# A retention and FFN kernel: the first 13 steps of pass 1 issued from a fixed list of small pieces

## The chip, the core and the metric

The kernel runs on one core of one Trainium2 chip. The metric is device time in microseconds (us) of one execution, lower is better. The kernel before takes 897.48 us (median of 3 runs, 896.96 to 897.90).

The engines are named as the profile names them: PE (TensorE; PEld is its weight load), DVE (VectorE), ACT (ScalarE), POOL (GpSimd) and SP (SyncE, which here only issues transfers). All times inside the profile are counted from the span's start.

## The reference, cut to what matters

```python
# B, H, S, D = 4, 8, 576, 64
scores = (q @ k.T) / sqrt(D)                        # retention, per batch and head
ret = scores * where(i >= j, gamma[h] ** (i - j), 0)
x = (ret @ v).transpose(0, 2, 1, 3).reshape(2304, 512)
h = x @ w_in                                        # 512 -> 2048
g = where(h >= 1, h, where(h <= -1, 0, (h + 1) ** 2 / 4))
x = g @ w_out                                       # 2048 -> 512
out = (x @ w_a) * (x @ w_b) @ w_out2                # 512 -> 1536 -> 512
```

q, k and v are float32. The weights are float64 and reach the kernel as 64-bit integers, so each weight tile is converted to float32 on the chip.

## The kernel before, in words

**Retention** runs over 18 chunks of 128 positions. For chunk c the kernel loads queries, keys and values (tile u, 1 MB in two transfers of 512 KB from SP, four buffers), scales the values by a decay on POOL (`prepare`), forms eight score products on PE into two PSUM banks and masks them on DVE into tile ret (`score`), then multiplies ret by the values into the bank po, adds the carried state's part to the same bank, and forms the chunk's own addition to the state in the bank pn (`output`). `evacuate` multiplies po by a decay into xf (DVE), rounds xf into the high part of x (ACT), adds pn to state (DVE, or an ACT copy where a batch begins) and subtracts to get the low part of x (DVE). A wait is written nowhere: it follows from tiles, buffers and banks.

**The first FFN layer** works on six blocks of 384 positions (three chunks each) and 16 slices of 128 hidden units, cut into three passes. Pass 1 covers slices 0 to 2 for block 0, 0 to 3 for block 1, 0 to 5 for the others. A step is one (block, slice): 12 products into the bank ph (`l1`), the activation on ACT, ACT, DVE, ACT, DVE (`act1`: t, t, t, high part of g, low part of g), and, one step later, 12 products into four accumulator banks (`l2`). Every product is done in three parts, high by high, low by high and high by low, on pairs of tiles that hold the two parts.

**Weights** come as raw tiles of 128 x 512 x 8 bytes (512 KB). `begin` does two ACT operations on a raw tile and two on DVE (L149, L152), `finish` one integer addition, and `split` an ACT copy (the high part) and a DVE subtraction (L168, the low part). The addition of the first two tiles is on DVE (L159, custom operation), that of the others on POOL (L159).

**The order.** Up to step 24 the five engines issue in the order in which the Python code calls these functions (`manual_schedule`); from step 25 on a scheduler decides. Before the change, a short sequence of calls does chunks 0 to 2 and the first tiles, and then the loop over steps calls `rounds_to` (whole chunks: score, then output and evacuate), the step's 12 products, `act1` with the next tile's conversion in its middle, and the previous step's `l2`. PSUM has four banks of tag ps, handed out in turn to s, s, po, pn and ph, so a product waits until the bank's last reader four allocations back is done; and four accumulator banks.

At the start, DVE zeroes a tile, four products on it run on PE, and the tables (con: masks and key decays; tab: four pieces of 6 KB) are loaded from the ACT queue; `table` spreads tab over the partitions with products and ACT copies into qdec.

Of the kernel before, what the change touches and what calls it, by code (L numbers as in the profile page):

```python
# [9 lines left out]
F32 = mybir.dt.float32  # L10
# [66 lines left out]
def retention_ffn_kernel(  # L77
# [29 lines left out]
    def mm(o, l, r, start, stop, goes_on=False):  # L107
        nc.tensor.matmul(o, l, r, start=start, stop=stop, skip_group_check=goes_on)  # L108
# [29 lines left out]
    def begin(raw, t=None):  # L138


        w = raw.bitcast(U32).rearrange("p (n t) -> p t n", t=2)
        low, high = w[:, 0, :], w[:, 1, :]
        r = raw.bitcast(I32).rearrange("p (n t) -> p t n", t=2)[:, 0, :]
        if t is None:
            t = conv_pool[0].tile([P, 512], F32, tag="conv", name="conv")
        tu = t.bitcast(U32)
        nc.scalar.activation(t, high.bitcast(F32), AF.Abs, scale=2.0 ** -112)
        nc.scalar.activation(r, low, AF.Copy, scale=2.0 ** -29)  # L148
        nc.vector.tensor_scalar(  # L149
            out=tu, in0=tu, scalar1=3, scalar2=None, op0=ALU.logical_shift_left  # L150
        )
        nc.vector.scalar_tensor_tensor(  # L152
            out=tu, in0=high, scalar=0x80000000, in1=tu, op0=ALU.bitwise_and, op1=ALU.bitwise_or
        )
        return t, r

    def finish(t, r, adder=None):
        ti = t.bitcast(I32)
        (adder or nc.vector).tensor_tensor(out=ti, in0=ti, in1=r, op=ALU.add)  # L159
        return t  # L160

    def convert(raw, t=None, adder=None):
        return finish(*begin(raw, t), adder)

    def split(t, pool):
        wt = pool.tile([P, 2, 512], F32R, tag="w", name="w")
        nc.scalar.copy(wt[:, 0, :], t)
        nc.vector.tensor_sub(wt[:, 1, :], t, wt[:, 0, :].bitcast(F32))  # L168
        return wt


    stream = []
# [235 lines left out]
    def score(c):  # L408

        mask = masks[len(parts_of(c)) - 1]  # L410
        t = units[c]
        f = rets[c] = a2.tile([P, 2, DM], F32, tag="ret", name="ret")
        s = [ps.tile([P, 512], F32, tag="ps", name=f"s{h}") for h in range(2)]
        for e in range(NCC):
            for h in range(2):
                rows = slice(D * h, D * h + D)
                mm(
                    s[h][:, P * e:P * e + P], t[rows, K0 + P * e:K0 + P * e + P],
                    t[rows, Q0 + P * e:Q0 + P * e + P], True, True,
                )  # L420
        for h in range(2):
            masked[0] = nc.vector.tensor_mul(  # L422
                f[:, h].rearrange("p (e i) -> p e i", e=NCC),
                s[h].rearrange("p (e i) -> p e i", e=NCC),
                mask.unsqueeze(1).to_broadcast([P, NCC, P]),
            )
# [36 lines left out]
    def evacuate(c, po, pn):  # L463

        x = get_x(c // CPB)
        o = slice(c % CPB * P, c % CPB * P + P)
        fv = po.rearrange("p (c i) -> p c i", c=NCC)
        f = a2.tile([P, DM], F32, tag="xf", name="xf").rearrange("p (c i) -> p c i", c=NCC)
        nc.vector.tensor_mul(f, fv, qdec[:, :, c * P % S:c * P % S + P])
        fv = f  # L470
        cast[0] = nc.scalar.copy(x[:, 0, :, o], fv)
# [8 lines left out]
        nc.vector.tensor_sub(x[:, 1, :, o], fv, x[:, 0, :, o].bitcast(F32))  # L480

    masked, cast = [None], [None]
    loaded, ready, scored, done = [0], [0], [0], [0]

    def load_next(limit):
# [17 lines left out]
    def output_next():  # L503

        c = done[0]
        load_next(c + CHUNKS)
        prepare_next(c + 3)
        evacuate(c, *output(c))
        done[0] += 1

    def rounds_to(n):
# [28 lines left out]
    def act1(ph, between=lambda: None):  # L540
        t = tpool.tile([P, TB], F32, tag="t", name="t")
        g = gpool.tile([P, 2, TB], F32R, tag="g", name="g")
        nc.scalar.activation(t, ph[:, :TB], AF.Relu, bias=0.5, scale=0.5)  # L543
        nc.scalar.activation(t, t, AF.Square)  # L544
        nc.vector.scalar_tensor_tensor(  # L545
            out=t, in0=t, scalar=1.0, in1=ph[:, :TB], op0=ALU.min, op1=ALU.max
        )
        between()
        anchor[:] = [
            nc.scalar.copy(g[:, 0, :], t),  # L550
            nc.vector.tensor_sub(g[:, 1, :], t, g[:, 0, :].bitcast(F32)),  # L551
        ]
# [4 lines left out]
    def accs(n):  # L557
        return [acc.tile([P, 512], F32, tag=f"acc{m}", name=f"acc{m}") for m in range(n)]

    def l2(step):  # L560
# [10 lines left out]
        if last:  # L571
            y_out(i, b)

    yin = {}
# [590 lines left out]
```

## Time and profile before

| | |
|---|---|
| median of 3 runs | 897.48 us (896.96 to 897.90) |
| the profiled execution's own time | 895.57 us |
| its span in the profile | 893.8 us |
| PE busy | 877.4 us, 98% of the span, 5716 products |
| PEld / DVE / ACT / POOL busy | 862.2 / 592.1 / 447.3 / 92.9 us |
| DMA over the span | 238.16 MB, 266 GB/s on average |

The profiled execution lies 1.9 us below the median of the runs, and 1.8 us of it lie around the span. Matmuls are pipelined, and the profile models their ends: a busy PE is not PE at its peak, and a product at half clock counts as busy too. The granted clock (PEclk) is 1.00 at 2.4 GHz and 0.50 at 1.2 GHz. An instruction's releaser is the one whose semaphore came last.

### The profile page before, as it was taken

The page shows a single profiled execution, that of the slowest core. Times are in us where ns is not written, and L with a number is a line of the kernel's source. Part 1 is how long each engine was busy: PE and PEld are TensorE (multiplying, and loading weights), DVE is VectorE, ACT ScalarE, POOL GpSimd, SP SyncE. Part 2 cuts the span into 40 slices and gives each one's busy share as a digit, 9 for nine tenths or more (in the row PEclk, how much of TensorE's full clock was granted, in tenths as well). Part 3 has the DMA queues.
Part 4 walks back from the last instruction along what each step waited for, and adds up shares of the span by engine and source line. Part 5 has one row for each costly group of instructions (what it writes and reads, how often), then busy time and mean ns, then how long its engine had stood idle before and what let it go on. Part 6 is the DMA issues. An engine that isn't in the chain of part 4 may idle for free.

```text
span 893.8 us, 15170 instructions
## 1 busy us (share of the span) xinstructions
PE 877.4 (98%) x5716; PEld 862.2 (96%) x5716; DVE 592.1 (66%) x1075; ACT 447.3 (50%) x903; POOL 92.9 (10%) x113
## 2 busy tenths in 40 slices
PE   8799999999999999999999999999999999999998
PEld 5689999999999999999999999999999999999998
DVE  3787776657777779877888966655245376245465
ACT  3444554456666577656667544443233353333253
POOL 1334433201100101111000000000000000000000
PEclk9799999999999999999999999999999999999999
DMA  8867644455787889998988997869556489857584
GB/s 325 310 245 274 246 170 173 154 188 204 246 312 286 297 278 311 304 382 321 341 292 290 406 398 265 283 224 338 192 200 213 141 282 405 335 179 235 171 285 157
DMA packets 81224, 238.16 MB, mean 266 GB/s; under 512 B 8408, under 2 KB 35160, under 8 KB 78848
## 3 DMA queue, kind: packets, MB, share of 16 engines
q1 hardware_dynamic: 71328, 196.64, 61.7%
q0 software_dynamic: 9664, 40.37, 13.1%
q8 instruction: 45, 0.74, 0.3%
q10 hardware_dynamic: 160, 0.19, 0.1%
q14 instruction: 27, 0.22, 0.1%
HBM read 175.83 MB, written 61.34 MB: 265 GB/s over the span
## 4 chain that ended last, share of the span: by engine, by line
PE 88%; DVE 5%; DMA 3%; issue 2%; ACT 2%; SPq 0%; POOL 0%; POOLq 0%; DVEq 0%; ACTq 0%
PE acc L108 31%; PE ph L108 21%; PE qx L108 16%; PE qy L108 8%; PE late L108 4%; PE qz L108 4%; PE po L108 2%; PE s L108 1%; DVE w L168 1%; DMA b<-yf 1%; DVE ret L422 1%; DVE conv L152 1%; DMA con<-in_const 1%; DMA tab<-in_const 0%; DMA yin<-y 0%
## 5 line engine op out<-in xcount | busy, mean ns | idle before, releaser
L108 PE MATMUL acc<-g,w 128*128 128x384 f32 x1296 | 247.1, 334 | 0.0
L108 PE MATMUL ph<-x,w 128*128 128x384 f32 x1152 | 223.6, 339 | 7.5 <-DVE ret L422 4.8
L108 PEld LDWEIGHTS acc<-g,w 128*128 128x128 f32 x1296 | 226.5, 188 | 0.1
L108 PEld LDWEIGHTS ph<-x,w 128*128 128x128 f32 x1152 | 203.5, 190 | 9.7 <-issue 5.5
L108 PE MATMUL qx<-tx,w 128*128 128x384 f32 x864 | 164.5, 334 | 0.5 <-DVE keep L688 0.5
L108 PEld LDWEIGHTS qx<-tx,w 128*128 128x128 f32 x864 | 151.0, 188 | 0.8 <-DVE keep L688 0.8
L666 ACT COPY keep<-qx 128x384 f32<-128x384 f32 x126 | 59.8, 481 | 141.9 <-PE qx L108 136.4
L545 DVE SCALAR_TENSOR_TENSOR t<-t,ph 128x384 f32<-128x384 f32 x96 | 52.9, 553 | 54.0 <-ACT t L544 53.6
L108 PE MATMUL qy<-tx,w 128*128 128x384 f32 x432 | 86.5, 335 | 0.0
L543 ACT ACTIVATE t<-ph 128x384 f32<-128x384 f32 x96 | 47.0, 489 | 72.0 <-PE ph L108 71.7
L108 PE MATMUL acc<-sp,w 128*128 128x384 f32 x432 | 77.5, 334 | 0.0
L108 PEld LDWEIGHTS qy<-tx,w 128*128 128x128 f32 x432 | 75.8, 188 | 0.6 <-ACT keep L666 0.3
L108 PEld LDWEIGHTS acc<-sp,w 128*128 128x128 f32 x432 | 75.1, 188 | 0.0
L550 ACT CAST g<-t 128x384 fp32r<-128x384 f32 x96 | 48.9, 510 | 39.4 <-DVE t L545 38.9
L551 DVE TENSOR_TENSOR g<-t,g 128x384 fp32r<-128x384 f32 x96 | 53.4, 556 | 21.3 <-ACT g L550 21.1
L759 DVE TENSOR_TENSOR sp<-gb,sp 128x768 fp32r<-128x768 f32 x42 | 40.2, 956 | 22.2 <-ACT sp L758 21.9
L544 ACT ACTIVATE t<-t 128x384 f32<-128x384 f32 x96 | 50.4, 526 | 2.6
L758 ACT CAST sp<-gb 128x768 fp32r<-128x768 f32 x42 | 35.2, 837 | 32.6 <-PE acc L108 18.8
L701 DVE TENSOR_TENSOR keep<-keep 128x384 f32<-128x384 f32 x36 | 20.1, 558 | 47.4 <-ACT keep L666 47.4
L148 ACT ACTIVATE raw<-raw 128x512 int32<-128x512 uint32 x68 | 45.6, 670 | 1.7 <-DMA raw<-in_moe_w_in 1.3
L108 PE MATMUL qz<-tx,w 128*128 128x384 f32 x216 | 43.4, 334 | 0.0
L688 DVE TENSOR_TENSOR keep<-qz,keep 128x384 f32<-128x384 f32 x36 | 20.1, 558 | 30.0 <-PE qz L108 29.1
(99 smaller groups left out, 993.0 us busy)
## 6 DMA issues: line engine op xcount, KB each, us to landing
w<-q SPq DMA_DIRECT2D x126, 512.0 KB, 5.3
q<-q SPq DMA_DIRECT2D x42, 512.0 KB, 5.8
w<-o SPq DMA_DIRECT2D x42, 512.0 KB, 4.6
u<-in_qkv SPq DMA_DIRECT2D x36, 512.0 KB, 6.1
x<-xd SPq DMA_DIRECT2D x12, 1536.0 KB, 8.0
raw<-in_moe_w_out POOLq DMA_DIRECT2D x18, 512.0 KB, 7.1
yin<-y SPq DMA_DIRECT2D x48, 192.0 KB, 4.2
xd<-x POOLq DMA_DIRECT2D x5, 1536.0 KB, 9.5
```

The lines of the kernel that those rows point to most:

```text
L108: nc.tensor.matmul(o, l, r, start=start, stop=stop, skip_group_check=goes_on)
L148: nc.scalar.activation(r, low, AF.Copy, scale=2.0 ** -29)
L543: nc.scalar.activation(t, ph[:, :TB], AF.Relu, bias=0.5, scale=0.5)
L544: nc.scalar.activation(t, t, AF.Square)
L545: nc.vector.scalar_tensor_tensor(out=t, in0=t, scalar=1.0, in1=ph[:, :TB], op0=ALU.min, op1=ALU.max)
L550: nc.scalar.copy(g[:, 0, :], t),
L551: nc.vector.tensor_sub(g[:, 1, :], t, g[:, 0, :].bitcast(F32)),
L666: nc.scalar.copy(t, o[:, :HT])
L688: nc.vector.tensor_add(self.c11, z[:, :HT], self.c11)
L701: nc.vector.tensor_add(self.c22, self.c22, self.s5)
L758: nc.scalar.copy(t[:, 0], b)
L759: nc.vector.tensor_sub(t[:, 1], b, t[:, 0].bitcast(F32))
```

## The change

The work of the first 13 steps (blocks 0, 1 and 2) and of the chunks that go with it is cut into pieces, and a table of 251 tokens says in which order the pieces are issued. Each engine gets its own pieces in that order. A token is a letter and a number: r and u load raw tile or chunk; V, S, P are prepare, score and output of a chunk; X, C, O are the three parts of evacuate (xf and the high part of x; state; low part of x); A, B, f or F, H, W are the parts of a weight tile's conversion (ACT pair; DVE pair; addition on POOL or DVE; high part; low part); L, T, U, G, J, Z are a step's first products, two ACT operations, DVE minimum and maximum, high part of g, low part of g, and second products; Q is table, Y the store of a block's accumulators, E the store of x. After the table the old loop goes on with step 13, with 12 chunks output, 13 scored, 14 prepared and 16 loaded. The loop of before stands at the same point when step 11's second products end.

Three things are changed besides: eight warm-up products instead of four, on a tile of which only one half is zeroed; tab is loaded from the POOL queue instead of ACT's; and the additions of tiles 0 and 1 go to POOL, those of tiles 8 and 10 to DVE.

```diff
-ON_POOL, BY_HAND = 12, 2
+ON_POOL = 12
+ORDER = """
+    r0 u0 r1 u1 u2 r2 u3 A0 B0 V0 S0 A1 B1 Q0 f0 S1 P0 u4 r3 X0 H0 V1 C0 W0 O0 S2 P1 u5
+    r4 r5 X1 V2 A2 C1 f1 B2 V3 O1 H1 f2 Q1 S3 P2 u6 r6 V4 X2 C2 S4 H2 O2 P3 u7 A3 W1 X3
...
 def begin(raw, t=None):
     nc.scalar.activation(t, high.bitcast(F32), AF.Abs, scale=2.0 ** -112)
     nc.scalar.activation(r, low, AF.Copy, scale=2.0 ** -29)
+        return t, high, r
+
+    def bits(t, high, r):
+
+        tu = t.bitcast(U32)
         nc.vector.tensor_scalar(
...
-    nc.vector.memset(warm.bitcast(F32), 0.0)
+    nc.vector.memset(warm[:, 0, :].bitcast(F32), 0.0)
     wacc = acc.tile([P, 512], F32, tag="acc0", name="wacc")
-    for _ in range(4):
-        mm(wacc, warm[:, 0, 0:P], warm[:, 1, :], True, True)
+    for _ in range(8):
+        mm(wacc, warm[:, 0, 0:P], warm[:, 0, :], True, True)
...
     for rows in rows_of:
-        nc.scalar.dma_start(tab[rows], const[rows, first:])
+        nc.gpsimd.dma_start(tab[rows], const[rows, first:])
...
-    load_next(2)
-    raws1.fetch_to(1)
-    load_next(3)
...
-    score_next()
-    begin_tile()
-    end_tile(1)
-    table(512, S + P // 2)
...
+    in_order = {
+        "u": load_chunk, "r": lambda k: raws1.fetch_to(k + 1),
+        "S": score, "V": prepare, "P": lambda c: chunk.update({c: evacuate(c, *output(c))}),
+        "X": lambda c: next(chunk[c]), "C": lambda c: next(chunk[c]), "O": lambda c: next(chunk[c]),
...
+    for token in ORDER.split():
+        in_order[token[0]](int(token[1:]))
+    by_order = sum(f1 - f0 for f0, f1 in GROUPS1[0][:3])
+    prev = steps[by_order - 1]
...
     for s, step in enumerate(steps[:last_by_hand]):
+        if s < by_order:
+            continue
```

**The load queue, first transfers (SP).** u is half a chunk, raw a weight tile. Before:

```order
L394 DMA u<-in_qkv 128x1024 x4
L135 DMA raw<-in_moe_w_in 128x4x128 [waits DMAHW1_49]
L394 DMA u<-in_qkv 128x1024 [waits DMAHW2_49]
L394 DMA u<-in_qkv 128x1024 [waits DMAHW3_49]
L135 DMA raw<-in_moe_w_out 128x512 [waits DMAHW4_49]
L394 DMA u<-in_qkv 128x1024 [waits DMAHW5_49]
```
Now:

```order
L148 DMA raw<-in_moe_w_in 128x4x128
L417 DMA u<-in_qkv 128x1024 x2
L148 DMA raw<-in_moe_w_out 128x512
L417 DMA u<-in_qkv 128x1024 x3
L417 DMA u<-in_qkv 128x1024 [waits DMAHW0_49]
L148 DMA raw<-in_moe_w_in 128x4x128 [waits DMAHW1_49]
```

The first weight tile moved ahead of the first chunk, the second ahead of chunk 1; a wait on a DMAHW semaphore is for an earlier transfer, and seven transfers now start without a wait where four did.

**PE around the first step's products (ph, 12 of them).** Before, they stand between the rest of the tables (acc, tab) and the scores of chunk 4 (s):

```order
L108 MATMUL acc_416<-tab 128x128
L108 MATMUL acc_417<-tab 128x128
L108 MATMUL acc_418<-tab 128x128
L108 MATMUL acc_419<-tab 128x128
L108 MATMUL ph<-x,w 128x384 [waits Activation_49]
L108 MATMUL ph<-x,w 128x384 [waits DVE_49] x2
L108 MATMUL ph<-x,w 128x384 x9
L108 MATMUL s_472<-u 128x128 [waits DMAHW0_49,PE_49]
L108 MATMUL s_473<-u 128x128 [waits DVE_49]
```
Now, between the output of chunk 3 and that of chunk 4:

```order
L121 MATMUL po<-ret,u 64x128 [waits DMAHW3_49,DVE_49,Pool_49]
L121 MATMUL po<-ret,u 64x128 x7
L121 MATMUL po<-u,state 64x128 [waits DVE_49] x2
L121 MATMUL po<-u,state 64x128 x6
L121 MATMUL pn<-u 64x64 [waits PE_49]
L121 MATMUL pn<-u 64x64 x7
L121 MATMUL ph<-x,w 128x384 [waits DVE_49,Activation_49]
L121 MATMUL ph<-x,w 128x384 [waits DVE_49]
L121 MATMUL ph<-x,w 128x384 x10
L121 MATMUL po<-ret,u 64x128 [waits DMAHW5_49,PE_49,Pool_49]
L121 MATMUL po<-ret,u 64x128 x7
```
The scores of chunk 4 and the output of chunk 3 (the po and pn rows above ph) moved ahead of the first step; the step is followed by chunk 4's output.

**DVE around chunk 6 (xf and state).** w is a weight tile's low part, t and g belong to the activation. Before: xf, state and the low part of x of chunk 5, the masked scores of chunk 7, then xf and state of chunk 6 with nothing between:

```order
L469 TENSOR_TENSOR xf<-po,qdec 128x512 [waits PE_49]
L479 TENSOR_TENSOR state<-pn,state 64x4x64 [waits PE_49]
L479 TENSOR_TENSOR state<-pn,state 64x4x64
L480 TENSOR_TENSOR x<-xf,x 128x4x128 [waits Activation_49]
L422 TENSOR_TENSOR ret<-s_714,con 128x512 [waits PE_49]
L422 TENSOR_TENSOR ret<-s_715,con 128x512 [waits PE_49]
L469 TENSOR_TENSOR xf<-po,qdec 128x512 [waits PE_49]
L479 TENSOR_TENSOR state<-pn,state 64x4x64 [waits DVE_49,PE_49]
L479 TENSOR_TENSOR state<-pn,state 64x4x64 [waits DVE_49]
```
Now the bits of tiles 5 and 6 stand in front of xf and behind it, and step 2's minimum and maximum (the first t row) ahead of state:

```order
L445 TENSOR_TENSOR ret<-s_689,con 128x512 [waits PE_49]
L445 TENSOR_TENSOR ret<-s_690,con 128x512 [waits PE_49]
L504 TENSOR_TENSOR x<-xf,x 128x4x128
L166 TENSOR_SCALAR conv<-conv 128x512
L169 SCALAR_TENSOR_TENSOR conv<-raw,conv 128x512 [waits DMAHW2_49,DVE_49]
L492 TENSOR_TENSOR xf<-po,qdec 128x512 [waits PE_49]
L166 TENSOR_SCALAR conv<-conv 128x512
L169 SCALAR_TENSOR_TENSOR conv<-raw,conv 128x512 [waits DMAHW5_49,DVE_49]
L570 SCALAR_TENSOR_TENSOR t<-t,ph 128x384 [waits Activation_49]
L502 TENSOR_TENSOR state<-pn,state 64x4x64 [waits PE_49]
L502 TENSOR_TENSOR state<-pn,state 64x4x64
```
The t row reads the ph bank of step 2, which is also the bank that chunk 6's pn is given on PE; that pn waits for the t row now.

## Rows read from the trace of the kernel before

**Rows 1.** Page, part 2: TensorE's granted clock in 40 slices.
```profile
PEclk9799999999999999999999999999999999999999
```
**Rows 2.** Busy time by stretch: from:to, us, PE, PEld, DVE, ACT, POOL, PEclk, DMA share, GB/s.
```profile
5.63:16.88 11.25, 10.85 (x72) 7.21 (x73) 3.25 (x5) 2.15 (x4) 3.12 (x3) 1.00 1.02 393
25.05:27.23 2.18, 0.01 (x2) 0.00 (x1) 1.46 (x4) 0.71 (x3) 0.03 (x1) 1.00 1.03 389
34.65:39.03 4.38, 0.00 (x1) 0.04 (x1) 4.35 (x7) 1.84 (x4) 2.10 (x2) 0.82 0.88 260
39.03:43.13 4.10, 4.10 (x12) 3.66 (x12) 2.49 (x5) 0.62 (x1) 2.33 (x3) 0.50 0.96 376
16.21:61.58 45.37, 38.06 (x466) 34.22 (x464) 37.52 (x61) 21.47 (x43) 15.54 (x13) 0.89 0.84 296
49.50:120.59 71.09, 70.84 (x680) 67.13 (x680) 53.73 (x83) 36.55 (x74) 26.67 (x27) 1.00 0.67 236
```
**Rows 3.** Timeline, first 17 us: start us, us, engine, line, operation, tiles, count, idle before.
```profile
2.00 2.08 PE L108 MATMUL wacc<-warm 128*128 128x512 f32 x4 [2.00 <-DVE warm L874]
5.63 2.08 PE L108 MATMUL s<-u 64*128 64x128 f32 x16 [1.56 <-DMA u<-in_qkv]
5.78 0.24 ACTq L885 DMA_DIRECT2D tab<-in_const  x1
...
10.12 2.07 PE L108 MATMUL acc<-tab 2*128 2x512 f32 x2 [0.39 <-DMA tab<-in_const]
...
16.21 0.69 DVE L469 TENSOR_TENSOR xf<-po,qdec 128x512 f32<-128x512 f32 x1 [0.70 <-PE po L108]
```
**Rows 4.** Timeline, first products on PE, and two in the dense stretch.
```profile
27.23 3.97 PE L108 MATMUL ph<-x,w 128*128 128x384 f32 x12 [2.17 <-ACT w L167]
...
61.58 2.35 PE L108 MATMUL ph<-x,w 128*128 128x384 f32 x12
...
81.27 2.24 PE L108 MATMUL ph<-x,w 128*128 128x384 f32 x12
...
83.35 2.25 PE L108 MATMUL acc<-g,w 128*128 128x384 f32 x12
```
**Rows 5.** Groups on DVE, 16.21 to 61.58: count, busy us, mean ns, idle before.
```profile
L168 DVE TENSOR_TENSOR w<-conv,w 128x512 fp32r<-128x512 f32 x6 | 7.8, 1296 | 1.4 <-ACT w L167 1.4
L422 DVE TENSOR_TENSOR ret<-s,con 128x512 f32<-128x512 f32 x12 | 7.7, 682 | 0.1
L152 DVE SCALAR_TENSOR_TENSOR conv<-raw,conv 128x512 uint32<-128x512 uint32 x7 | 4.9, 693 | 0.2
L469 DVE TENSOR_TENSOR xf<-po,qdec 128x512 f32<-128x512 f32 x7 | 4.8, 683 | 0.7 <-PE po L108 0.7
L480 DVE TENSOR_TENSOR x<-xf,x 128x512 fp32r<-128x512 f32 x6 | 4.2, 693 | 1.5 <-ACT x L471 1.4
L479 DVE TENSOR_TENSOR state<-pn,state 64x256 f32<-64x256 f32 x8 | 3.3, 417 | 0.1
L149 DVE TENSOR_SCALAR conv<-conv 128x512 uint32<-128x512 uint32 x7 | 2.9, 421 | 0.0
L545 DVE SCALAR_TENSOR_TENSOR t<-t,ph 128x384 f32<-128x384 f32 x3 | 1.7, 554 | 4.5 <-ACT t L544 4.5
L551 DVE TENSOR_TENSOR g<-t,g 128x384 fp32r<-128x384 f32 x3 | 1.6, 548 | 0.0
L159 DVE CUSTOM_DVE_ANT_0 conv<-raw,conv 128x1024 uint16<-128x1024 uint16 x2 | 1.4, 684 | 0.0
```
**Rows 6.** Groups on POOL, 0 to 120.59, same columns.
```profile
L401 POOL TENSOR_TENSOR u<-u,con 128x512 f32<-128x512 f32 x15 | 18.6, 1242 | 18.7 <-DMA u<-in_qkv 18.7
L159 POOL TENSOR_TENSOR conv<-conv,raw 128x512 int32<-128x512 int32 x11 | 16.0, 1456 | 59.8 <-DVE conv L152 49.3 <-ACT g L550 8.2 <-issue 1.7
```
**Rows 7.** Timeline on POOL: the decay product of chunk 3.
```profile
18.35 1.04 POOL L401 TENSOR_TENSOR u<-u,con 128x512 f32<-128x512 f32 x1 [2.85 <-DMA u<-in_qkv]
```
**Rows 8.** DMA issues, 49.5 to 120.59: count, KB each, median us to landing.
```profile
y<-yst POOLq DMA_DIRECT2D x8, 192.0 KB, 4.9
```

More of the change, by code (lines that the diff above doesn't have):

```diff
@@ L37 @@
 Q0, K0, R0, V0 = 0, 512, 1024, 1536
+ORDER = """
+    r0 u0 r1 u1 u2 r2 u3 A0 B0 V0 S0 A1 B1 Q0 f0 S1 P0 u4 r3 X0 H0 V1 C0 W0 O0 S2 P1 u5
+    r4 r5 X1 V2 A2 C1 f1 B2 V3 O1 H1 f2 Q1 S3 P2 u6 r6 V4 X2 C2 S4 H2 O2 P3 u7 A3 W1 X3
+    L0 C3 W2 B3 T0 P4 u8 r7 E0 U0 f3 X4 O3 A4 S5 V5 H3 B4 C4 W3 G0 f4 L1 P5 u9 r8 r9 J0
+    T1 H4 A5 A6 Z0 X5 C5 V6 W4 O4 U1 S6 G1 L2 J1 S7 O5 T2 V7 P6 B5 X6 L3 A7 B6 U2 T3 C6
+    f5 r10 V8 f6 r11 u10 H5 H6 L4 G2 U3 B7 Z1 J2 G3 T4 f7 P7 u11 r12 V9 W5 U4 V10 A8 L5
+    X7 O6 W6 A9 J3 S8 C7 G4 Z2 T5 U5 B8 P8 u12 J4 Y0 E1 B9 S9 G5 X8 C8 V11 F8 r13 O7 O8
+    L6 f9 r14 H7 Z3 T6 Z4 H8 S10 L7 U6 V12 T7 W7 L8 G6 H9 U7 J5 T8 L9 T9 U8 A10 W8 Z5 J6
+    B10 P9 u13 W9 L10 G7 Z6 X9 U9 L11 E2 T10 F10 G8 Y1 J7 U10 C9 G9 V13 S11 O9 P10 u14
+    X10 Z7 T11 J8 Z8 U11 H10 J9 C10 W10 L12 S12 A11 Z9 G10 P11 u15 r15 T12 B11 J10 X11
+    f11 G11 Z10 U12 H11 J11 Z11 C11 G12 J12 W11 O10 O11
+"""
 def constants(H, D, S):
@@ L162, in convert, with split_hi, split_lo, split @@
     def convert(raw, t=None, adder=None):
-        return finish(*begin(raw, t), adder)
-    def split(t, pool):
+        return finish(*bits(*begin(raw, t)), adder)
+    def split_hi(t, pool):
         wt = pool.tile([P, 2, 512], F32R, tag="w", name="w")
         nc.scalar.copy(wt[:, 0, :], t)
+        return t, wt
+    def split_lo(t, wt):
         nc.vector.tensor_sub(wt[:, 1, :], t, wt[:, 0, :].bitcast(F32))
         return wt
+    def split(t, pool):
+        return split_lo(*split_hi(t, pool))
     stream = []
@@ L421, in score @@
         for h in range(2):
-            masked[0] = nc.vector.tensor_mul(
+            nc.vector.tensor_mul(
                 f[:, h].rearrange("p (e i) -> p e i", e=NCC),
@@ L469, in evacuate @@
         nc.vector.tensor_mul(f, fv, qdec[:, :, c * P % S:c * P % S + P])
[L470 to L471 removed]
+        yield
+        nc.scalar.copy(x[:, 0, :, o], f)
         for h in range(2 if pn is not None else 0):
@@ L479, in evacuate @@
                 nc.vector.tensor_add(to, of, to)
-        nc.vector.tensor_sub(x[:, 1, :, o], fv, x[:, 0, :, o].bitcast(F32))
-    masked, cast = [None], [None]
+        yield
+        nc.vector.tensor_sub(x[:, 1, :, o], f, x[:, 0, :, o].bitcast(F32))
+        yield
     loaded, ready, scored, done = [0], [0], [0], [0]
@@ L507, in output_next @@
         prepare_next(c + 3)
-        evacuate(c, *output(c))
+        for _ in evacuate(c, *output(c)):
+            pass
         done[0] += 1
@@ L538, in l1, with act1_parts @@
         return ph, [(o, l, r, i == 0, i == len(ops) - 1) for i, (o, l, r) in enumerate(ops)]
-    def act1(ph, between=lambda: None):
+    def act1_parts(ph):
         t = tpool.tile([P, TB], F32, tag="t", name="t")
-        g = gpool.tile([P, 2, TB], F32R, tag="g", name="g")
         nc.scalar.activation(t, ph[:, :TB], AF.Relu, bias=0.5, scale=0.5)
         nc.scalar.activation(t, t, AF.Square)
+        yield
         nc.vector.scalar_tensor_tensor(
@@ L547, in act1 @@
         )
+        yield
+        g = gpool.tile([P, 2, TB], F32R, tag="g", name="g")
+        hi = nc.scalar.copy(g[:, 0, :], t)
+        yield g
+        anchor[:] = [hi, nc.vector.tensor_sub(g[:, 1, :], t, g[:, 0, :].bitcast(F32))]
+        yield
+    def act1(ph, between=lambda: None):
+        parts = act1_parts(ph)
+        next(parts)
+        next(parts)
         between()
[L549 to L552, printed above, removed]
+        g = next(parts)
+        next(parts)
         return g
@@ L558, in accs, with l2 @@
         return [acc.tile([P, 512], F32, tag=f"acc{m}", name=f"acc{m}") for m in range(n)]
-    def l2(step):
+    def l2(step, out=True):
         i, b, f, first, last = step
@@ L570, in l2 @@
             used(("o", f))
-        if last:
+        if last and out:
             y_out(i, b)
@@ L900, in begin_tile @@
         if i < 2 * GROUPS1[1][0][1] and free() > len(begun):
-            begun.append(begin(raws1.next()))
-            if i >= BY_HAND:
-                begun[-1] = finish(*begun[-1], nc.gpsimd), None
+            begun.append(finish(*bits(*begin(raws1.next())), nc.gpsimd))
             raws1.more()
@@ L909, in end_tile @@
             key = stream[made[0]][0]
-            t, r = begun.pop(0)
-            weights[key] = split(t if r is None else finish(t, r), take(key))
+            weights[key] = split(begun.pop(0), take(key))
             made[0] += 1
@@ L951, in needed, with first_product @@
         return place["o", step[2]] + 1
+    half, parts, chunk, gen = {}, {}, {}, {}
+    in_order = {
+        "u": load_chunk, "r": lambda k: raws1.fetch_to(k + 1),
+        "S": score, "V": prepare, "P": lambda c: chunk.update({c: evacuate(c, *output(c))}),
+        "X": lambda c: next(chunk[c]), "C": lambda c: next(chunk[c]), "O": lambda c: next(chunk[c]),
+        "Q": lambda k: table(*((0, 512), (512, S + P // 2))[k]),
+        "A": lambda k: half.update({k: begin(raws1.next())}),
+        "B": lambda k: half.update({k: bits(*half[k])}),
+        "F": lambda k: half.update({k: finish(*half[k])}),
+        "f": lambda k: half.update({k: finish(*half[k], nc.gpsimd)}),
+        "H": lambda k: half.update({k: split_hi(half[k], take(stream[k][0]))}),
+        "W": lambda k: weights.update({stream[k][0]: split_lo(*half.pop(k))}),
+        "T": lambda k: next(gen[k]), "U": lambda k: next(gen[k]),
+        "G": lambda k: gs.update({steps[k]: next(gen[k])}), "J": lambda k: next(gen[k]),
+        "Z": lambda k: l2(steps[k], False), "Y": lambda b: y_out(0, b),
+        "E": lambda b: nc.gpsimd.dma_start(xd[b], xt[b].bitcast(F32)),
+    }
+    def first_product(k):
+        i, b, f, *_ = steps[k]
+        ph, ops = l1(xt[b], weights["i", f])
+        for o in ops:
+            mm(*o)
+        gen[k] = act1_parts(ph)
+    in_order["L"] = first_product
+    for token in ORDER.split():
+        in_order[token[0]](int(token[1:]))
+    by_order = sum(f1 - f0 for f0, f1 in GROUPS1[0][:3])
+    prev = steps[by_order - 1]
+    loaded[0], ready[0], scored[0], done[0] = 16, 4 * CPB + 2, 4 * CPB + 1, 4 * CPB
+    made[0] = 2 * max(f1 for _, f1 in GROUPS1[0][:3])
     last_by_hand = sum(f1 - f0 for f0, f1 in GROUPS1[0][:-1])
     for s, step in enumerate(steps[:last_by_hand]):
+        if s < by_order:
+            continue
         i, b, f, first, last = step
```

15 lines of the change are left out of this document (removed).

## The prediction

> **What bounds the kernel now.** I read the granted clock first [rows 1]: one slice at 9, one at 7, all others at full. So whatever the first 13 steps lose is lost early. The table of stretches [rows 2] says where. From 49.5 to 120.59 us, where step 11's second products end and where the change hands over to the old loop, PE is busy 70.84 of 71.09 us at clock 1.00, and DVE 53.73. Nothing is to be had there. Before that PE stands still twice, for 2.18 us ahead of step 0's products and for 4.38 us ahead of step 1's, while DVE is busy 4.35 of those 4.38. After both gaps PE works at 1.2 GHz: the clock is 0.50 from 39.03 to 43.13, and step 0's 12 products take 3.97 us where later ones take 2.24 [rows 2, 4]. The start is slow too: the first 16 score products take 2.08 us [rows 3], and 5.63 to 16.88 is spent on two scores, the first tables and one output, with DMA at 393 GB/s and share 1.02, that is, full [rows 2].
>
> So until about 61 us the kernel waits for DVE, and DVE waits for what PE has not yet done. From the first xf of chunk 0 (16.21 [rows 3]) to step 3's first products (61.58 [rows 4]) DVE is busy 37.52 of 45.37 us [rows 2]; the groups of that stretch [rows 5] show the 7.85 us of idle, 4.5 of them ahead of the activation's t, which waits for ACT and so for PE's late products.
>
> **The change, part by part.**
>
> *Start.* A weight tile of 512 KB now goes ahead of chunk 0; at 393 GB/s that is 1.3 us, so the first scores start at 6.9 instead of 5.63. Eight warm-up products instead of four take twice 2.08 us [rows 3] and, begun half a microsecond earlier because half the tile is zeroed, end near 5.7: the wait for chunk 0 covers them, and if the chunk came at 5.6 they would cost 0.1. What they do to the clock no row shows: below, a gain of nothing; above, the start at full clock (second rival). I take nothing, because four of them followed by a gap of 1.56 us left the scores at half speed [rows 3], and the new gap is 1.2 us. The tables went out on ACT as late as 5.78 and PE waited 0.39 us for the last one at 10.12 [rows 3]; from POOL they are issued at once, and even at the 4.9 us of POOL's 192 KB stores [rows 8] they land before the scores end at 9. That saves 0.4. The order score 0, tables, score 1, output 0 is kept, so the first xf starts at 16.21 + 1.3 - 0.4 = 17.1. POOL's four issues lie before its first decay product, which waits for data.
>
> *The load queue.* Up to chunk 4 the same bytes are loaded, only in another order, and DMA is full. The third weight tile is ahead of chunk 3 now, so that chunk's decay product goes from 18.35, where it waited 2.85 us for the transfer [rows 7], to about 19.7. Chunk 3's output is not due before 26, as 9.6 us of DVE's list lie between the first xf and the state it reads; this costs nothing unless DVE gets there sooner.
>
> *DVE up to step 3.* Between chunk 0's xf and the t of step 2 the new list has the same 7 xf, 12 masked scores, 6 low parts of x, 8 state additions and 3 t. It lacks two pairs of bit operations (tiles 0 and 1, done earlier, beside the waits of the start): 2 x (0.69 + 0.42) = 2.2 us; the two custom additions, which went to POOL: 1.4; one w, 0.69; and one g, 0.55 [rows 5]. That is 4.8 less: 32.7 us busy. In this I keep today's waits for POOL: six w took 7.8 us where the other operations with two SBUF inputs take 0.69, so 7.8 - 4.1 = 3.7 us were lost to it.
>
> *DVE's idle time.* The list puts chunk 3's output and chunk 4's scores ahead of step 0 and chunk 4's output behind it, so that PE has work while DVE finishes x and the weights, and t is no longer waited for in front of a full queue. I take 3 us of idle instead of 7.85. The ends: 1 (only the waits for PE at the first xf and scores remain), and 7.85 (nothing won). One hole I can see: chunk 6's pn must wait for the t of step 2, and on DVE one pair of bits, xf, another pair and t stand between chunk 5's x and that point, 1.1 + 0.68 + 1.1 + 0.55 = 3.4 us, about 3 of which PE has nothing for. It is inside the sum, since the sum goes along DVE.
>
> *Sum.* t of step 2 ends at 17.1 + 32.7 + 3.0 = 52.8. Then come pn's 16 small products, a quarter of 2.08 [rows 3], 0.5, and step 3 starts at 53.3. Before it started at 61.58, but with step 1's second products done, which take 83.35 - 81.27 = 2.08 [rows 4] and come after step 3 now. So 59.5 against 53.3: **6.2 us earlier**. The rest up to 120.59 is the same work, PE-bound before with DVE idle for 17 of 71 us, so the lead is kept. The additions of tiles 8 and 10 on DVE (0.7 each) and the pieces' new order lie in that slack. On POOL the store of block 0's x now waits for its last part, with tile 3's addition behind it; tile 3 is first used after step 3 starts, so that is covered. What follows step 13 is unchanged work.
>
> The profiled execution would go from 895.57 to 889.4. Against the median of the runs, which is 1.9 above it, 897.48 - 6.2 = **891.3 us**.
>
> **A rule against the change.** In 16.21 to 61.58 POOL did four additions and DVE lost 3.7 us; the new list has five additions and seven decay products of POOL in that place. The Trainium skill (SBUF — State Buffer, "Who interferes with whom") says that a DVE instruction with two SBUF inputs and a GpSimd instruction that reads SBUF exclude each other for a whole instruction, whoever starts first. By that rule x, g and the second bit operation are exposed as w is. The rows agree for w (1296 ns on average against 693 for x [rows 5]); that x was spared is a matter of when POOL started. This gives the third rival.
>
> **The rivals.**
>
> 1. *The forecast*, 891.3.
>
> 2. *The clock rises at the start and the list leaves DVE no holes.* With full clock from 6.9 the scores are done by 8, and chunk 1's first half, three transfers of 1.3 us later, lets score 1 start at 11; xf starts near 13, 4 us sooner. Half of that survives, as chunk 3 is not in before 19.7. With 1 us of idle instead of 3 the gain is 6.2 + 2 + 2 = 10.2: 887.3. For it: DVE's operations differ by under 2% within a group, but for w, so a list without holes can be kept to. Against it: the waits of [rows 3].
>
> 3. *POOL holds DVE up (slower).* Seven decay products of 1.24 us and five additions of 1.46 [rows 6] are 16 us. If each falls on a DVE operation and holds it for its whole length, 16 instead of 3.7 us are lost: 12.3 more, 6.1 slower, 903.6. It decides from (3.7 + 6.2) / 16, 62% of POOL's time, on. Against it: masked scores, xf, t and state read PSUM, and DVE has 18 exposed operations among some 60.
>
> 4. *The clock falls in a hole.* If PE's 3 us at chunk 6's pn act as the 4.38 us did before step 1, steps 3 and 4 run at half clock, 2 us each: gain 2.2, 895.3; with 1 us more lost to POOL it is no change. That the list doesn't do what it says, idle staying at 7.85, gives 6.2 - 4.9 = 1.3, 896.2, and belongs here.
>
> **How the numbers follow.** Chances: forecast 0.59, second 0.17, POOL 0.09, fallen clock or no holes closed 0.15. A measurement of this kernel can tell about 0.2%, 1.8 us, from no change. Faster by more than that are the first two and half of the last, 0.83; within it the other half, 0.08; slower 0.09. The range leaves out POOL's case at the top and at the bottom what lies beyond the second rival: 886.3 to 896.5.
>
> **What would show it.** Right: step 3's products start at 52 to 55 us with step 1's second products behind them; the stretch from chunk 0's xf to there has some 33 us of DVE work; granted clock at 0.50 nowhere between 20 and 50; step 11's second products end near 114; the rest is as long as before. Wrong: w, x and g with means over 1.2 us (third rival), 0.50 around chunk 6's pn (fourth), or the lead at step 13 gone by the end, which nothing above provides for.

## The result, and the profile after

The changed kernel takes **884.58 us** (median of 4 runs, 883.87 to 885.88) against 897.38 us for the kernel before in the same comparison (4 runs): ratio 0.9859, 95% interval 0.9842 to 0.9876. That is 12.8 us earlier. The forecast was 6.2 us and 891.3; the result lies below its range, which ended at 886.3. The direction was right and the size was not.

The profiled execution of the changed kernel took 885.88 us, with a span of 884.0, so the two spans differ by 9.8 us only (893.8 to 884.0). The difference lies behind the handover, where both kernels run the same code: 773.2 us before and 776.1 here, and between 772.5 and 776.1 in the traces of the changed kernel and its variants (774.7 when the changed kernel was run again). So I compare stretches ahead of the handover, and medians of runs for the whole. (The profiled execution of one later kernel, the second with chunk 0 first, was a disturbed one, and its trace is not read.)

The page's totals and its row of the granted clock:

```profile
PE 873.8 (99%) x5720; PEld 859.5 (97%) x5720; DVE 587.3 (66%) x1075; ACT 447.1 (51%) x903; POOL 93.4 (11%) x117
PEclk9999999999999999999999999999999999999999
```

No slice is below 9 any more; before, one was at 7 [rows 1]. The busy time by stretch, same columns as [rows 2]: the start, chunk 0's xf to the end of step 2's t, step 3 to the handover, and the rest:

```profile
6.96:15.08 8.12, 8.12 (x64) 6.17 (x65) 4.64 (x7) 3.81 (x7) 3.56 (x4) 1.00 1.03 403
15.08:50.86 35.78, 35.78 (x479) 33.25 (x478) 33.55 (x54) 20.96 (x42) 16.63 (x15) 1.00 1.01 377
46.44:107.93 61.49, 61.49 (x544) 58.20 (x540) 44.28 (x74) 30.16 (x62) 20.68 (x23) 1.00 0.66 229
107.93:884.00 776.07, 769.03 (x4661) 763.85 (x4660) 507.99 (x945) 391.10 (x792) 52.83 (x71) 1.00 0.75 267
```

In the first three, PE is busy for every microsecond. Its waits from 6 us to the handover (engine, tile, line, releaser: us in total, times, longest) are a single row, the wait for the first chunk:

```profile
PE s L121 <- DMA u<-in_qkv: 1.7, 1, 1.7
```

The same view of the kernel before:

```profile
PE ph L108 <- DVE ret L422: 4.8, 2, 4.4
PE ph L108 <- ACT w L167: 2.2, 1, 2.2
PE s L108 <- DMA u<-in_qkv: 1.6, 1, 1.6
PE acc L108 <- DMA tab<-in_const: 0.4, 1, 0.4
PE po L108 <- DVE state L479: 0.2, 1, 0.2
```

The timeline of the changed kernel at the places that the prediction spoke of (columns as in [rows 3]):

```profile
6.96 2.08 PE L121 MATMUL s<-u 64*128 64x128 f32 x16 [1.71 <-DMA u<-in_qkv]
...
8.96 2.09 PE L121 MATMUL acc<-tab 2*128 2x512 f32 x8
...
15.08 0.69 DVE L492 TENSOR_TENSOR xf<-po,qdec 128x512 f32<-128x512 f32 x1 [0.70 <-PE po L121]
...
27.34 2.36 PE L121 MATMUL ph<-x,w 128*128 128x384 f32 x12
...
32.67 2.36 PE L121 MATMUL ph<-x,w 128*128 128x384 f32 x12
...
44.18 1.29 DVE L445 TENSOR_TENSOR ret<-s,con 128x512 f32<-128x512 f32 x2 [1.62 <-PE s L121]
...
45.88 0.63 PE L121 MATMUL pn<-u 128*64 128x64 f32 x16
...
46.44 4.43 PE L121 MATMUL ph<-x,w 128*128 128x384 f32 x24
...
50.32 0.54 DVE L570 SCALAR_TENSOR_TENSOR t<-t,ph 128x384 f32<-128x384 f32 x1
...
107.93 1.16 PE L121 MATMUL s<-u 64*128 64x128 f32 x16
```

The last row is the handover: step 11's second products are done and the next scores start. In the kernel before, that row stood at 120.59. So the lead there is **12.66 us**. Step 0 starts at 27.34, as late as before (27.23 [rows 4]); but nothing stands still in front of it or behind it, and its products take 2.36 us instead of 3.97.

**Where the 12.7 came from.** Rows of the kernel before that the sum needs:

```profile
7.64 2.08 PE L108 MATMUL acc<-tab 2*128 2x512 f32 x6
...
12.12 2.08 PE L108 MATMUL s<-u 64*128 64x128 f32 x16
...
39.03 4.18 PE L108 MATMUL ph<-x,w 128*128 128x384 f32 x12 [4.38 <-DVE ret L422]
43.13 1.71 PE L108 MATMUL s<-u 64*128 64x128 f32 x16
...
120.59 1.16 PE L108 MATMUL s<-u 64*128 64x128 f32 x16
```

From the first scores to the handover PE took 120.59 - 5.63 = 114.96 us before, and 107.93 - 6.96 = 100.97 now: 14.0 shorter, less 1.3 for the later start. The rows account for 13.7 of the 14.0. The waits ahead were 4.8 + 2.2 + 0.4 + 0.2 = 7.6. Slow products behind the two gaps cost 3.97 - 2.36 = 1.6 in step 0 (granted clock 0.56 from 27.23 to 31.13), 4.18 - 2.36 = 1.8 in step 1 (0.50), and 1.71 - 1.16 = 0.55 in the scores behind it (0.64 from 43.13 to 44.77). The first table products took from 7.64 to 12.12 before and 8.96 to 10.98 now: 4.48 against 2.02, and without the 0.39 of waiting 2.1.

### The profile page after: what moved, and what is told of

It reads as the page before. It is cut to its first block, busy times and chain, and to the rows that moved or that the text cites. A ratio compares the mean times of both kernels' runs of the same rounds, so it can differ in the third digit from the quotient of the medians.

```text
span 884.0 us, 15204 instructions
## 1 busy us (share of the span) xinstructions
PE 873.8 (99%) x5720; PEld 859.5 (97%) x5720; DVE 587.3 (66%) x1075; ACT 447.1 (51%) x903; POOL 93.4 (11%) x117
## 3 DMA queue, kind: packets, MB, share of 16 engines
q0 software_dynamic: 9792, 40.40, 13.1%
## 4 chain that ended last, share of the span: by engine, by line
PE 84%; issue 10%; DMA 3%; DVE 2%; ACT 1%; POOL 0%; SPq 0%; POOLq 0%
PE acc L121 31%; PE ph L121 21%; PE qx L121 14%; PE qy L121 7%; PE po L121 4%; PE qz L121 3%; DMA b<-yf 3%; PE s L121 3%; PE late L121 2%; PE pn L121 1%; DMA u<-in_qkv 1%; DVE yin L623 0%; DVE stage L176 0%; DVE stage L169 0%; ACT w L184 0%
## 5 line engine op out<-in xcount | busy, mean ns | idle before, releaser
L121 PE MATMUL ph<-x,w 128*128 128x384 f32 x1152 | 219.6, 336 | 0.1
L121 PEld LDWEIGHTS ph<-x,w 128*128 128x128 f32 x1152 | 200.5, 188 | 1.7 <-DVE t L570 0.4
L700 ACT COPY keep<-qx 128x384 f32<-128x384 f32 x126 | 59.5, 479 | 141.1 <-PE qx L121 135.9
L792 ACT CAST sp<-gb 128x768 fp32r<-128x768 f32 x42 | 35.2, 837 | 32.7 <-PE acc L121 18.8
```

The lines of the kernel that those rows point to most:

```text
L700: nc.scalar.copy(t, o[:, :HT])
L792: nc.scalar.copy(t[:, 0], b)
```

## The experiments

My theory after the result had three parts: PE has other products to run while DVE finishes block 0's x; DVE does the first weight tiles' work in its idle time at the start; the start itself is shorter by the table's pieces that come together. The rival for each was that it is hidden anyway. Edits are to the changed kernel unless said. "Handover" is the start of the same scores row as above; the changed kernel has it at 107.93, and at 108.12 when it was run again; losses are counted from the mean of the two, 108.03. Ratios are to the kernel before on the same chip.

**The changed kernel once more**, as the yardstick: no edit.

> The changed kernel once more, unchanged, so that the variants beside it are compared on the same chip: 0.986 of the kernel before, as in the first comparison (0.9859).

Ratio 0.9871 (0.9856 to 0.9886). In the trace the first xf is at 15.22.

**Fill for PE taken away.** Chunk 4's scores and chunk 3's output go behind step 0's products again, and with these tokens their work on DVE and ACT (the masks, xf and the high part of x):

```diff
-... V4 X2 C2 S4 H2 O2 P3 u7 A3 W1 X3
-    L0 C3 W2 B3 T0 P4
+... V4 X2 C2 H2 O2 u7 A3 W1
+    L0 S4 P3 X3 C3 W2 B3 T0 P4
```

> The changed kernel with the scores of chunk 4 and the output of chunk 3 issued behind step 0's first products, as before the change. Theory (the gain is that PE has products to do while DVE finishes x of block 0): PE stands still for some 2 to 3.5 us ahead of step 0's products, the time of the 3.5 us of products moved, and perhaps falls to 1.2 GHz once; 2 to 6 us slower. Rival (the gain lies elsewhere, in less DVE work and the start): under 1 us slower.

Ratio 0.9912 (0.9888 to 0.9935), handover 112.89: 4.9 us of the lead are gone. PE's waits from 6 us up to there:

```profile
PE ph L121 <- ACT x L494: 2.2, 1, 2.2
PE s L121 <- DMA u<-in_qkv: 1.8, 1, 1.8
PE s L121 <- DVE t L570: 0.8, 1, 0.8
PE ph L121 <- DVE x L504: 0.3, 1, 0.3
```

The timeline on PE at step 0:

```profile
25.30 0.55 PE L121 MATMUL ph<-x,w 128*128 128x384 f32 x1 [2.23 <-ACT x L494]
26.16 3.43 PE L121 MATMUL ph<-x,w 128*128 128x384 f32 x11 [0.31 <-DVE x L504]
```

The gap of 2.2 us ahead of step 0 is back, and behind it the slow products (3.43 for eleven; granted clock 0.59 from 25.30 to 29.50). With this one move undone the kernel looks, at this place, like the kernel before. The 4.9 are the three new waits, 3.3, and 0.55 + 3.43 - 2.36 = 1.6 for the slow products. So the fill is shown to be worth 4.9 in these traces.

**Weight tiles converted late.** The work of tiles 0 and 1 on ACT and DVE (A, B) leaves the waits of the start and goes behind chunks 0 and 1; what follows from it (their high and low parts H and W, and tile 2's first pieces) moves back with it:

```diff
-    r0 u0 r1 u1 u2 r2 u3 A0 B0 V0 S0 A1 B1 Q0 f0 S1 P0 u4 r3 X0 H0 V1 C0 W0 O0 S2 P1 u5
-    r4 r5 X1 V2 A2 C1 f1 B2 V3 O1 H1 f2 Q1 S3 P2 ...
+    r0 u0 r1 u1 u2 r2 u3 V0 S0 Q0 S1 P0 u4 r3 X0 V1 C0 O0 A0 B0 f0 S2 P1 u5
+    r4 r5 X1 A1 B1 V2 C1 f1 O1 H0 A2 B2 V3 W0 H1 f2 Q1 S3 P2 ...
```

> The changed kernel with the conversion of weight tiles 0 and 1 moved out of the waits of the start: their bits come behind the low part of chunk 0's x and behind chunk 1's xf, as in the kernel before, instead of before 12 us. 2.2 us of DVE's work and the low parts of the tiles move into the stretch before step 1. Theory (two things are needed, products to fill PE with and DVE work brought forward; DVE has about 2 us of slack, as 4.8 us more work cost 3): 0.5 to 2 us slower, with PE waiting ahead of step 0. Rival (DVE's early work is worth nothing, the fill is all): no change.

Ratio 0.9938 (0.9921 to 0.9954), handover 112.44: 4.4 us gone, more than I had expected. PE's waits:

```profile
PE s L121 <- DVE ret L445: 2.9, 1, 2.9
PE s L121 <- DMA u<-in_qkv: 1.7, 1, 1.7
PE po L121 <- DVE state L502: 0.2, 1, 0.2
```

Here PE does not wait for a weight but for the masked scores, and DVE is busy 2.83 of the 2.90 us from 24.90 to 27.80: DVE's list is the queue, and what is put into it before step 0 pushes back what stands behind. Step 0 starts at 31.85 instead of 27.34:

```profile
27.80 1.75 PE L121 MATMUL s<-u 64*128 64x128 f32 x16 [2.87 <-DVE ret L445]
...
31.85 2.35 PE L121 MATMUL ph<-x,w 128*128 128x384 f32 x12
```

Unlike the gaps of 2.2 and 4.4 us in the kernel before, this one of 2.87 left the granted clock at 1.00, and step 0's products took their 2.35 us.

**Both together.** The edits of the last two in one kernel.

> late_bits and late_fill together: tiles 0 and 1 converted late, and the scores of chunk 4 and the output of chunk 3 behind step 0's products. Theory (both have to do with what DVE has ready when step 0 and step 1 start, so they add up or more): 5.5 to 9 us slower than the changed kernel, with PE gaps ahead of steps 0 and 1 and 1.2 GHz behind them, as in the kernel before. Rival (the fill's 5 us already hold all of it): 5 us slower.

Ratio 0.9970 (0.9959 to 0.9981), handover 117.40: 9.4 us gone, which is 4.9 + 4.4 and 0.1. They add up: with the conversion late, too, the fill is worth 117.40 - 112.44 = 5.0, so it does not need the early conversion. Whole runs tell less. By the ratios the three losses against the yardstick are 3.7, 6.0 and 8.9 us, each known to 2 or 3 us. PE's longest wait is now ahead of step 0:

```profile
PE ph L121 <- ACT x L494: 4.7, 1, 4.7
```

**The fill alone, in the kernel before.** Chunk 3's and 4's scores are called earlier and chunk 3's output goes ahead of step 0, nothing else:

```diff
     output_next()
     begin_tile()
+    score_next()
     output_next()
+    score_next()
     end_tile()
-    score_next()
+    output_next()
     begin_tile()
     end_tile(1)
```

> The kernel before with one move of the change alone: scores of chunk 4 and output of chunk 3 are issued ahead of step 0's products (and the scores of chunk 3 ahead of chunk 2's output), so that PE has them to do while DVE finishes block 0's x and weight tile 0. Theory (the gain is products moved into PE's gaps): the gap of 2.18 us ahead of step 0 goes, and the products at half speed behind it; DVE still has the same work ahead of step 1, so part of the gap of 4.38 us stays: 2 to 5 us faster, 892.5 to 895.5. Rival (only the whole list, or the start, gains): within 1 us of the kernel before.

Ratio 1.0022 (1.0012 to 1.0032): slower, 1.7 us by the medians, where my theory had expected a gain. Handover at 123.27, 2.7 us later; but in this trace the table's last piece was late as well (PE waited 1.5 us for it, and the first xf is at 17.23 instead of 16.21). Three of PE's waits:

```profile
PE ph L108 <- ACT w L167: 6.9, 2, 6.2
PE acc L108 <- DMA tab<-in_const: 1.5, 1, 1.5
...
PE s L108 <- DVE ret L422: 0.8, 1, 0.8
```

The gap ahead of step 0 shrank from 2.17 to 0.70 us, and the one ahead of step 1 grew from 4.38 to 6.2, now for its weight tile: in these calls the last part of that tile's conversion, `end_tile(1)`, stands behind the moved output of chunk 3 and its evacuation. So in the old order this move only moved the gap. This is the reverse of the last three runs: taken from the finished list, each part costs more than 4 us; put into the old order, this one costs 1.7 instead of winning 5. That it is the place of tile 1's conversion that makes the difference is my reading of the wait; no run moves it by itself.

**More work on DVE.** The xf multiplication of chunks 0 to 6 is done twice, with the same output, which is 7 x 0.68 = 4.8 us of DVE more:

```diff
-        nc.vector.tensor_mul(f, fv, qdec[:, :, c * P % S:c * P % S + P])
+        for _ in range(2 if c < 7 else 1):
+            nc.vector.tensor_mul(f, fv, qdec[:, :, c * P % S:c * P % S + P])
```

> The changed kernel with the multiplication po by decay into xf done twice for chunks 0 to 6 (the second repeats the first): 7 x 0.68 = 4.8 us more work on DVE before step 3. Forecast's theory (DVE's list sets when step 3 starts): 4.8 us slower, 889.4. Theory now (PE never waits for DVE in this stretch; step 3 started 4.4 us before DVE's t of step 2 that the forecast put ahead of it): DVE has slack of a few us, so under 2 us slower.

Ratio 0.9892 (0.9871 to 0.9912), handover 111.17, 3.1 us later. Of 4.8 us DVE could take some 1.7 without PE noticing. Between the two expectations: DVE is not idle in this stretch, but PE has a little work in stock.

**Additions on DVE.** Those of tiles 0 and 1 go back from POOL:

```diff
-    ... B1 Q0 f0 S1 P0 ... C1 f1 B2 ...
+    ... B1 Q0 F0 S1 P0 ... C1 F1 B2 ...
```

> The changed kernel with the additions of tiles 0 and 1 on DVE again: 1.4 us more on DVE, 2.9 us less on POOL, so less of the waits between the two. Both theories: within 1 us of the changed kernel; by the forecast's DVE sum up to 1.4 us slower, less what POOL no longer takes.

Ratio 0.9860 (0.9833 to 0.9886), handover 108.73: no difference in time that the runs can tell. The 1.4 us that the forecast took for it lie within that stock.

**Half the warm-ups.**

```diff
-    for _ in range(8):
+    for _ in range(4):
```

> The changed kernel with four warm-up products instead of eight. Theory: no change within 1 us, since the first scores take 2.08 us with eight as with four, and PE reaches the full rate near 16 in both. Rival (the eight products raise the clock earlier and that is where the unforeseen gain comes from): 2 us slower or more, 886.6.

Ratio 0.9872 (0.9855 to 0.9889): no difference. The scores started at 7.60 in that trace, the first xf at 15.73, and the handover was 108.74, later by as much.

**The tables.** Three kernels: the changed one with tab on the ACT queue again, the kernel before with tab on the POOL queue, and the changed one with the fourth piece of the table made late (issued by SP behind weight tile 1).

```diff
-        nc.gpsimd.dma_start(tab[rows], const[rows, first:])
+        nc.scalar.dma_start(tab[rows], const[rows, first:])
```

In the kernel before it is the reverse of this. The late piece, with D a token that issues it:

```diff
-    r0 u0 r1 u1 ...
+    r0 u0 r1 D3 u1 ...
...
-    for rows in rows_of:
+    for rows in rows_of[:3]:
```

> The changed kernel with one thing undone: tab is loaded from the ACT queue again. Theory (in the changed kernel PE never waits after 9 us, so the start counts in full; the four table products run at the same time when all four pieces are there, 2.09 us together, while before the fourth came late and took another 2.07 us alone): the first xf goes from 15.08 to about 17.1, 2.0 us slower, 886.6 us. Rival (the forecast's price: only the wait of 0.39 us counts): 0.4 us slower or nothing, 885.0.

> The kernel before with this one part of the change alone: tab from the POOL queue. Theory: the first xf comes 2 to 2.4 us earlier (about 14), and of that 1 to 2 us reach the end, since chunks 2 and 3 (14.4 and 18.35 in the trace of before) are waited for: 895.4 to 896.4. Rival (0.39 us is all): 897.0.

> The changed kernel with the fourth table piece loaded from SP behind weight tile 1, so that it lands near 10 as in the kernel before. Theory (PE has no wait after 7 us in the changed kernel, so a late start counts in full): three table products run at 9.0, the fourth alone from about 10 to 12, the first xf comes 1 to 2 us later, and the end 1 to 2 us later. Rival (the start is not what sets the end; DVE and the arrival of chunks 2 and 3 take the loss in, as they took in the 1.5 us that the earlier tables won in the kernel before): under 0.6 us.

All three ended at no difference. With tab on ACT the ratio is 0.9857 (0.9841 to 0.9873): the table's pieces were hardly late there (all eight products took 2.35 us without a wait), the first xf was at 15.52 and the handover at 108.39, so this run did not test the cost. It does show that POOL's queue is not what brings the pieces together in the changed kernel: with the scores starting at 7.12 instead of 5.63 and the last piece issued at 4.7 instead of 5.78, ACT's queue does it nearly as well. In the kernel before, POOL's queue does bring the first xf forward, from 16.21 to 14.70, but the ratio is 0.9995 (0.9984 to 1.0005) and the handover 120.08; three of PE's waits there:

```profile
PE ph L108 <- DVE ret L422: 5.5, 3, 4.1
...
PE po L108 <- DVE state L479: 1.4, 1, 1.4
```

Of the 1.5 us, 0.5 are left at the handover; the rest is lost to longer waits for DVE's state (1.4 where it was 0.2) and for its masked scores (5.5 where it was 4.8). The late fourth piece delayed the first xf to 15.89 only, and the handover to 108.64; the ratio is 0.9886 (0.9867 to 0.9905), not to be told from the yardstick's. Against the changed kernel's profiled execution (first xf 15.08, handover 107.93) the first xf came 0.4 us later with tab on ACT (15.52), 0.65 with half the warm-ups and 0.8 with the late piece, and the handover 0.5, 0.8 and 0.7. So in these traces a delay of the first xf reaches the handover nearly whole in the changed kernel, and a gain of it goes mostly lost in the kernel before, to the waits behind it. The whole runs cannot tell differences of under 1 us.

**Chunk 0 loaded first.** Its two transfers go ahead of weight tile 0:

```diff
-    r0 u0 r1 u1 u2 r2 u3 A0 B0 V0 S0 A1 B1 Q0 f0 S1 P0 ...
+    u0 r0 u1 r1 u2 r2 u3 A0 B0 V0 S0 A1 B1 Q0 f0 S1 P0 ...
```

In a second kernel the pieces of ACT and DVE follow that order too:

```diff
-    r0 u0 r1 u1 u2 r2 u3 A0 B0 V0 S0 A1 B1 Q0 f0 S1 P0 ...
+    u0 r0 u1 r1 u2 r2 u3 V0 S0 A0 B0 Q0 f0 S1 A1 B1 P0 ...
```

> The changed kernel with the first four loads swapped pairwise: chunk 0, weight tile 0, chunk 1, weight tile 1. Theory (PE is dense from the first scores on, DVE has slack): scores start at 5.6 instead of 6.95 and the whole chain moves up by about 1.3 us, 883.3, unless chunk 3 at 18.9 becomes a wait. Rival (the list is fitted to its load order; DVE then waits for tile 0): no change or up to 1 us slower.

> The changed kernel with chunk 0 loaded ahead of weight tile 0 and chunk 1 ahead of weight tile 1, and with the list's first tokens put in the same order, so that DVE masks chunk 0's scores ahead of tile 0's bits (in the run with the loads alone swapped the scores began at 5.64 but the first xf came at 15.92, behind tile 0's bits). Theory: the first xf comes near 14.2 and the end is up to 1 us earlier than the unchanged one beside it. Rival (chunk arrival and DVE set the pace up to 25 us): no difference.

Ratios 0.9873 (0.9856 to 0.9890) and 0.9869 (0.9849 to 0.9889): no difference. The timeline of the first shows what held it up:

```profile
5.64 1.16 PE L121 MATMUL s<-u 64*128 64x128 f32 x16 [0.40 <-DMA u<-in_qkv]
...
9.14 0.43 DVE L166 TENSOR_SCALAR conv<-conv 128x512 uint32<-128x512 uint32 x1 [7.73 <-ACT conv L159]
...
10.21 1.28 DVE L445 TENSOR_TENSOR ret<-s,con 128x512 f32<-128x512 f32 x2
```

The scores are done at 6.8, but DVE's list has tile 0's bits ahead of the mask, and tile 0 now comes later: the first xf is at 15.92 and the handover at 108.62. The second kernel takes the bits out of the way and gained nothing either; what limits that one is not shown. No version of the study beat the changed kernel beyond the noise.

## Why the prediction was right and wrong

**The failed step is step 3's start at 53.3 in the sum, and in it the rule that chunk 6's pn, and so step 3, waits for DVE's t of step 2.** Step 3 started at 46.44, 6.9 us earlier and 4.4 ahead of the end of that t: from the first scores to the handover PE waits for nothing. Of that 13.1 us of lead (59.5 - 46.44), 12.7 are left at the handover. Two errors make up the 6.9:

- **4.9 us: pn of chunk 6 does not wait for the t of step 2.** The forecast had four banks handed out in turn, so that pn would get the bank that step 2's ph still held; it said so in the prediction and the text ahead of it. The timeline has pn at 45.88, straight behind the products in front of it, and that t at 50.32. In the program as built, ph of step 2 has bank 7 and pn of chunk 6 bank 5, and pn's wait counts to the first masked scores of chunk 7, the pair that starts at 44.18. The t of step 2 stands behind pn in the list of tokens, so at that point ph's bank still has a reader to come, and here the pool gave out one whose readers all stand before. I had reasoned "four allocations back" without looking which DVE instruction the wait counts to. With that wait the 3 us hole at pn falls too, and what the fourth rival hung on it. The second run of the changed kernel has the same order (pn at 46.06, t at 50.51). No run puts the wait back, so its price is read from these traces and not from a comparison.
- **2.0 us: the first xf at 15.08 instead of 17.1.** The order of the terms was right, their sizes not. The first scores started at 6.96 (forecast 6.9). But the late table piece cost the kernel before more than the 0.4 us of waiting: its two products at 10.12 took another 2.07 us [rows 3], while now all four pieces take 2.09 us together. Weight tile 0 ahead of chunk 0 costs 1.3, as forecast, and the table gives back 2.5, not 0.4. POOL's queue is worth only some 0.3 of that: from the first scores to the first xf 10.58 us pass in the kernel before, 8.12 in the changed one and 8.40 in the changed one with tab on ACT. That this is a gain for the whole was not shown by itself: in the kernel before, where POOL's queue brought the first xf 1.5 us forward, no gain was left.

**What held.** *DVE's sum* is the part that came out: from the first xf to the end of step 2's t it took 35.78 us (forecast 52.8 - 17.1 = 35.7), with 33.55 busy (32.7) and 2.2 idle (3). The sum was right for DVE; the mistake was to let PE wait for its end. The groups of DVE in that stretch, as in [rows 5]:

```profile
L445 DVE TENSOR_TENSOR ret<-s,con 128x512 f32<-128x512 f32 x12 | 7.7, 682 | 1.8 <-PE s L121 1.6
L504 DVE TENSOR_TENSOR x<-xf,x 128x512 fp32r<-128x512 f32 x6 | 5.4, 900 | 0.0
...
L169 DVE SCALAR_TENSOR_TENSOR conv<-raw,conv 128x512 uint32<-128x512 uint32 x5 | 4.2, 838 | 0.2
...
L188 DVE TENSOR_TENSOR w<-conv,w 128x512 fp32r<-128x512 f32 x5 | 3.5, 702 | 0.1
L166 DVE TENSOR_SCALAR conv<-conv 128x512 uint32<-128x512 uint32 x5 | 3.0, 595 | 0.0
L577 DVE TENSOR_TENSOR g<-t,g 128x384 fp32r<-128x384 f32 x2 | 2.2, 1102 | 0.0
L570 DVE SCALAR_TENSOR_TENSOR t<-t,ph 128x384 f32<-128x384 f32 x3 | 1.6, 548 | 0.0
```

*The wait for t* went, as forecast: 4.5 us of idle ahead of it before [rows 5], 0.0 now. *POOL's share* (third rival) did not grow. The prediction set five additions and seven decay products of POOL against four additions before; the trace of before has five additions and six decay products in that stretch, 14.6 us, against 17.1 for six and seven now, so POOL's work there grew much less than that count says. Against the means in [rows 5], x lost 6 x 0.21, the second bit operation 5 x 0.145, the first 5 x 0.17 and g 2 x 0.55, while w is back at 702 ns: 4.0 us in all, where the forecast kept 3.7. The Trainium skill (SBUF — State Buffer, "Who interferes with whom") puts x, g and the second bit operation among the exposed ones, and these rows agree; the loss has moved from w to them. *The clock* (fourth rival) fell nowhere: the three stretches read 1.00, and there is no gap in them. *The warm-ups* are worth nothing that the run with four could tell. *The additions of tiles 0 and 1* were worth 1.4 in the sum and nothing in time that could be told.

**The second rival** (887.3) came nearer to the time than the forecast, but by luck: the first scores still take 2.08 us, so the clock did not rise at the start; DVE's idle time was 2.2 us, not 1; and the earlier xf came from the table. Its premise of under 2% of spread within a group of DVE's was also a little narrow: in the trace of before the masks take 673 to 693 ns and the state additions 403 to 428.

**How the gain divides.** Fill for PE 4.9, early conversion 4.4, by removal and in single traces, and 9.4 for both removed together. The remaining 3.3 of the 12.7 are not separated; the shorter start is in them, at most 1.1 us as far as the first xf goes (16.21 to 15.08).

## What to carry to other kernels

A wait on a buffer that a pool hands out is read from the built program, from which instruction the wait counts to, not from the order of allocations: one wrongly assumed wait was 4.9 of the 6.9 us that were missed. When two engines feed each other from fixed lists, a move in one list may only move the gap: the same move of PE's work was worth 4.9 us in the finished list and cost 1.7 in the old order. And a gap can cost more than its length: behind 2.2 and 4.4 us of standing still the next products ran at granted clocks of 0.50 to 0.64, another 4.0 us; behind 2.87 us, in the run with late conversion, the clock stayed at 1.00.

## What the runs showed of the hardware that was not expected

**Four products of two rows take the time of one.** The table's four pieces lie on partitions 0, 32, 64 and 96. All four, eight instructions, took 2.09 us in the changed kernel; in the kernel before the one late piece took 2.07 by itself [rows 3]. The Trainium skill (TensorE: Matmul & The Clock Gate, "Part 3: Packing small matmuls — row/col tiling") says that products on different row groups of the array run at once; these rows agree. So a piece that comes after the others are done costs a whole product more, besides the wait. One that comes while they run costs less: with the late fourth piece in the changed kernel all eight took 2.67 us.

**The granted clock of the first stretch doesn't show the speed.** The stretch from 6.96 to 15.08 reads 1.00, but the 16 score products in it take 2.08 us, where the same 16 take 1.16 at 107.93, 1.8 times as long. In two variants (chunk 0 first, and the fill taken away) they took 1.16 right at the start, and the next 16 took 2.08 at a granted clock that now reads 0.50; in the others the first 16 took 2.08. The warm-ups were the same in both and in most of the others; what decides it stays open.

**A DVE operation with one tensor input was stretched too.** The first bit operation takes 0.42 us alone, 0.97 at 10.36 and 1.30 at 47.65, both times beside one of POOL's additions. The forecast had not counted it among the exposed ones.
